# Turning the expert rows on VectorE in 32x32 squares instead of on TensorE

## The chip, the cores and the metric

The kernel runs on one core of a Trainium2 chip. The metric is device time in microseconds (us) of one execution; the kernel before takes 2286.07 us, the median of three runs (2285.0 to 2286.5). Lower is better. All data are float32 in HBM; the products on TensorE (PE) are split products, in which each operand is written as a high part (rounded to the type fp32r) and a low part (what the rounding left), and three of the four partial products are summed.

## The reference

The first half is an attention without a softmax over 8 batches of 2496 tokens, the second a mixture of 8 experts over all 19968 tokens, each sent to one expert:

```python
# attention: u, v (8, 2496, 256), z (8, 2496, 64)
scores = scale * np.matmul(z, z.transpose(0, 2, 1))     # scale = 1 / 2496
x = u * np.matmul(np.maximum(scores, 0.0) ** 2, v)       # then (19968, 256)
# mixture of experts: w_gate (256, 8), w1 (8, 256, 1024), w2 (8, 1024, 256)
logits = x @ w_gate + modality_bias[modality_id]
e_idx = np.argmax(logits, axis=1)
probs = np.exp(logits - logits.max(-1, keepdims=True)); probs /= probs.sum(-1, keepdims=True) + 1e-09
gate_w = probs[np.arange(N), e_idx]
for e in range(8):
    mask = e_idx == e
    out[mask] = gate_w[mask, None] * (np.maximum(x[mask] @ w1[e], 0.0) @ w2[e])
```

## The kernel before

**Phase 1** (from the start to about 1357 us) does the attention in 400 steps: 8 batches, 5 chunks of up to 512 query tokens in each, 10 steps of 256 key tokens in each chunk. A step's scores go through PE (`s`, L265), ScalarE (ACT) twice (`r`, L267 and L273), are split into `ah` (L280, on ACT or on VectorE (DVE), as a planner chooses) and `al` (L289, DVE), and are multiplied by `v` on PE (`acc`, L305). A finished chunk leaves its PSUM banks (L347, L351), is turned and multiplied by `u`, and stands in a buffer `x` of 512 rows of 258 numbers (256 values, the gate, the token number). DVE then makes the chunk's 32 dot products with `w_gate` (`logits`, L403: 128x256 each, two to a piece, 16 pieces). After a batch's last logits its routing follows, and each 128 rows of `x` are scattered by an indirect DMA from GpSimd (POOL) to their expert's rows in the HBM buffer `xs` (L516).

The order of DVE and ACT in phase 1 is made in Python, before the run, by a planner: `queue(first step, due step, pieces)` hands it pieces with the engine and an assumed cost, and in each step it places what is due and, where its clock for the engine has room, what is not yet due. The pieces that are due decide at which step the logits stand before or behind the next `al`.

**Phase 2** runs 39 full tiles of 512 tokens of one expert, numbered -4 to 34, then a quarter tile of 128 tokens and a short end that is left by branches. SyncE (SP) fetches a tile's rows from `xs` into `xg` by one DMA (L757: 128 partitions of four rows of 258 numbers, 4128 B each), and an expert's weights by two more (L775, L779), which ACT and DVE split (L795, L799). The expert products need the rows with their 256 values on the partitions: `turn` (L819) turns them on PE by eight products with the identity into two PSUM banks (`pt`), and `part_rows` makes `xh` (ACT, L827) and `xl` (DVE, L828) from these. In tile t this is done for tile t+1, behind step f = 1 (f = 5 in the tiles before 0).

A tile has eight steps f. `up(t, f)` is six products (L984) into a bank `ph`; ACT makes `hh` from it (L988), DVE `hl` (L989). Two steps later `down(t, f)` multiplies these by the second weights into four banks `po` (L997 with `hh`, L998 with `hl`, once for each 128 tokens). So step f puts on PE `up(f)` and four pairs of `down(f-2)`; behind step 7 come `down(6)` and `down(7)` for each bank, and `finish` scales the banks by the gate (ACT L1012, DVE L1014) and scatters them to the output (POOL L1016). In phase 2 the order on each engine is the order in which the code issues.

The seam between the phases: tile -4 starts as soon as its rows and weights are split, while the last chunk of batch 7 is still being evacuated, turned, multiplied (L351, L372), given its logits, routed and scattered between the steps of tiles -4 to -1. The tiles from 0 on may be fetched only after the last of these scatters.

## Time and profile before

| | |
|---|---|
| median of three runs | 2286.07 us |
| profiled execution, own time | 2288.12 us |
| its span, first to last instruction | 2286.2 us |
| PE busy | 2263.1 us, 99% |
| DVE busy | 1756.6 us, 77% |
| ACT busy | 1584.1 us, 69% |
| POOL busy | 364.6 us, 16% |
| 16 DMA engines, mean of the HBM traffic | 101 GB/s |
| mean granted TensorE clock | 0.997 of full |

Busy time is the time in which an engine executes; times are of the one profiled execution. The granted clock in a row of windows is a share of the full 2.4 GHz. In a list of waits "a <- b" means that the work named a could not start before b had ended. A number in brackets at the end of a timeline row is the time that the engine stood idle before it and what it waited for; a row without one followed the row before it on its engine at once. Matmuls of one bank overlap in a timeline: from one start to the next is what one costs.

### The profile page before, as it was taken

Reading aid. Unit: us, or ns where it says so; the run is one execution under the profiler, and the core shown is the slowest. Engines: PE = TensorE matmul, PEld = TensorE weight load, DVE = VectorE, ACT = ScalarE, POOL = GpSimd, SP = SyncE. Lnnn points to the kernel's source line nnn. Section 1 sums busy time; section 2 is a strip of 40 time slices with the busy share of each in tenths; the row PEclk is TensorE's granted clock in tenths of the full one; section 3 lists DMA queues with packets and bytes.
Section 4 is the critical chain, followed back from the end, with each engine's and each line's share of the span. In section 5 each row is a group of like instructions: output and inputs, shape, how many; then the busy total and the mean of one; then the engine's idle time right before and its main releaser. Section 6 shows DMA issues by size and latency. Waiting matters only on the chain.

```text
span 2286.2 us, 44695 instructions
## 1 busy us (share of the span) xinstructions
PE 2263.1 (99%) x17194; PEld 1945.6 (85%) x17194; DVE 1756.6 (77%) x4544; ACT 1584.1 (69%) x1957; POOL 364.6 (16%) x349
## 2 busy tenths in 40 slices
PE   9999999999999999999999999999999999999996
PEld 7789889889899899889888888888888888888885
DVE  6889989989989889889889997555555565656563
ACT  7888888888888888888888863545444544545452
POOL 0000210210220210210210413212121212121111
PEclk9999999999999999999999999999999999999998
DMA  9612112112112112112111122434343444434340
GB/s 303 226 33 66 47 47 78 38 53 71 41 52 70 41 60 62 52 50 64 49 43 33 58 93 91 169 118 148 129 145 133 136 141 131 146 124 154 116 155 22
DMA packets 101743, 216.62 MB, mean 95 GB/s; under 512 B 15472, under 2 KB 63216, under 8 KB 96656
## 3 DMA queue, kind: packets, MB, share of 16 engines
q1 hardware_dynamic: 86432, 172.48, 23.1%
q0 software_dynamic: 15088, 41.21, 4.9%
q8 instruction: 136, 2.23, 0.4%
q14 instruction: 87, 0.71, 0.1%
HBM read 168.23 MB, written 62.19 MB: 101 GB/s over the span
## 4 chain that ended last, share of the span: by engine, by line
PE 85%; DVE 10%; issue 3%; ACT 1%; DMA 0%; POOL 0%; DVEq 0%; POOLq 0%; ACTq 0%
PE acc L305 36%; PE ph L984 18%; PE po L997 12%; PE s L265 10%; PE po L998 6%; DVE spare L403 4%; DVE al L289 3%; PE pt L819 1%; DVE vl L240 1%; DVE ah L280 1%; PE po L381 1%; DVE x L351 1%; ACT r L267 1%; ACT r L273 0%; DVE x L391 0%
## 5 line engine op out<-in xcount | busy, mean ns | idle before, releaser
L267 ACT ACTIVATE r<-s 128x1024 f32<-128x1024 f32 (+1 forms) x400 | 403.8, 1010 | 199.5 <-PE s L265 194.8
L289 DVE TENSOR_TENSOR al<-r,ah 128x1024 fp32r<-128x1024 f32 (+1 forms) x360 | 431.3, 1198 | 102.0 <-ACT ah L280 86.7
L403 DVE SCALAR_TENSOR_TENSOR spare<-x,wgb 128x256 f32<-128x256 f32 x1280 | 462.8, 423 | 1.0
L305 PE MATMUL acc<-ah,vh 64*128 64x512 f32 (+1 forms) x3120 | 454.4, 384 | 0.9 <-DVE ah L280 0.9
L997 PE MATMUL po<-w,hh 128*128 128x512 f32 x1256 | 450.1, 393 | 0.0
L988 ACT ACTIVATE hh<-ph 128x512 fp32r<-128x512 f32 x312 | 186.8, 599 | 378.3 <-PE ph L984 374.0
L305 PE MATMUL acc<-ah,vl 64*128 64x512 f32 (+1 forms) x3120 | 445.6, 383 | 0.0
L305 PE MATMUL acc<-al,vh 64*128 64x512 f32 (+1 forms) x3120 | 444.5, 382 | 0.0
L984 PE MATMUL ph<-xh,w 128*128 128x512 f32 x1248 | 439.8, 398 | 0.5 <-DVE hl L989 0.3
L273 ACT ACTIVATE r<-r 128x1024 f32<-128x1024 f32 (+1 forms) x400 | 416.8, 1042 | 3.3
L989 DVE SCALAR_TENSOR_TENSOR hl<-ph,hh 128x512 fp32r<-128x512 f32 x312 | 215.6, 691 | 248.4 <-ACT hh L988 246.9
L516 POOL DMA_INDIRECT xs<-x,sloti x160 | 204.4, 1278 | 1028.1 <-DVE x L514 946.2
L305 PEld LDWEIGHTS acc<-ah,vh 64*128 64x128 f32 x3120 | 324.0, 184 | 48.3 <-ACT x L347 2.9
L305 PEld LDWEIGHTS acc<-al,vh 64*128 64x128 f32 x3120 | 324.7, 184 | 41.8
L305 PEld LDWEIGHTS acc<-ah,vl 64*128 64x128 f32 x3120 | 319.7, 185 | 45.1
L265 PE MATMUL s<-zm 64*128 64x512 f32 (+1 forms) x2400 | 352.6, 387 | 2.3 <-ACT r L267 2.3
L998 PE MATMUL po<-w,hl 128*128 128x256 f32 x1256 | 350.7, 279 | 0.0
L280 ACT CAST ah<-r 128x1024 fp32r<-128x1024 f32 (+1 forms) x289 | 294.8, 1020 | 0.0
L997 PEld LDWEIGHTS po<-w,hh 128*128 128x128 f32 x1256 | 235.4, 187 | 56.1
L984 PEld LDWEIGHTS ph<-xh,w 128*128 128x128 f32 x1248 | 234.0, 188 | 56.9 <-DVE hl L989 2.3
L265 PEld LDWEIGHTS s<-zm 64*128 64x128 f32 x2400 | 241.7, 185 | 32.9 <-ACT r L267 4.3
L1016 POOL DMA_INDIRECT out_dram<-y,ids x157 | 153.2, 976 | 720.5 <-DVE y L1014 694.8
(152 smaller groups left out, 1975.2 us busy)
## 6 DMA issues: line engine op xcount, KB each, us to landing
...
```

Source lines behind the costliest of these rows:

```text
L265: nc.tensor.matmul(out=s[:, t, :w], lhsT=lhs, rhs=mv[halves[t], ql, :w], start=n == 0, stop=n == 2)
L267: nc.scalar.activation(out=r[:, :, :w], in_=s[:, :, :w], func=AF.Relu, scale=INV)
L273: nc.scalar.square(out=a[:, :, :w], in_=a[:, :, :w])
L280: copy(out=ah[:, :, :w], in_=st_a[g][:, :, :w])
L289: nc.vector.tensor_tensor(out=al[:, :, :w], in0=a[:, :, :w], in1=ah[:, :, :w].bitcast(F32), op=ALU.subtract)
L305: nc.tensor.matmul(out=acc[b, c][r][dh][:, :w], lhsT=V[b, k // J][y][halves[r], k % J, dh * P:(dh + 1) * P], rhs=x[halves[r], k % 2, :w], ...
L403: nc.vector.scalar_tensor_tensor(out=spare[:, k % 2, :], in0=x[:, j, 0:D], scalar=1.0, in1=wgb[:, e, :], op0=ALU.mult, op1=ALU.mult, accum ...
L516: nc.gpsimd.indirect_dma_start(out=xs, out_offset=bass.IndirectOffsetOnAxis(ap=RT[b]["sloti"][:n, k:k + 1], axis=0), in_=x[:n, j, :], in_o ...
L984: nc.tensor.matmul(out=ph, lhsT=lhs, rhs=rhs[:, k, :], start=n == 0, stop=n == 3 * KD - 1)
L989: nc.vector.scalar_tensor_tensor(out=hl, in0=ph, scalar=0.0, in1=hh.bitcast(F32), op0=ALU.max, op1=ALU.subtract)
L997: nc.tensor.matmul(out=po[j], lhsT=hh[:, s], rhs=both, start=f == 0, stop=False, skip_group_check=True)
L998: nc.tensor.matmul(out=po[j][:, 0:D], lhsT=hl[:, s], rhs=w[:, 0, :], start=False, stop=f == KF - 1, skip_group_check=True)
```

## The change

The eight products with the identity, their two PSUM banks and the split from PSUM go. A tile's rows are now fetched by four DMAs, each of 32 partitions by 16 by 64 numbers (2048 pieces of 256 B in all), so that the 32x32 squares of the row matrix lie where one transposition of 128x1024 numbers by DVE, which turns each square in itself, brings the values onto the partitions (`turn_blocks`); a fifth DMA brings the gates and token numbers (512 pieces of 8 B). ACT makes the high part (`part_high`, 128x1024), DVE the low part (`part_low`, 128x1024). The values then stand on the partitions in another order, and the first weights are laid into HBM in that order, by two DMAs for an expert instead of one. The tile t+1 is turned behind step 6 of tile t and split behind step 7 (4 and 5 in tile -3). There are two buffers of `xg` instead of three, four of gates, seven of `x` instead of six, two of logits instead of one; the four PSUM banks that `ph` and `pt` shared two and two all belong to `ph`. In phase 1 the logits of a chunk are due by half a step each from step 8 of the next chunk on (before: step 6, and for a batch's last chunk a third of a step each from step 5; that stays for batch 6's last chunk and batch 7's second). The small tile `tt` is filled at the start. The diff, cut:

```diff
-            nc.sync.dma_start(out=w1s[e], in_=w1[e].rearrange("(k p) f -> p k f", p=P))
+            for k in range(KD):
+                nc.sync.dma_start(
+                    out=w1s[e, :, k, :].rearrange("(b q) f -> b q f", q=BLK),
+                    in_=w1[e].rearrange("(b k q) f -> k b q f", k=KD, q=BLK)[k],
+                )
...
-            x = rows.tile([P, J, XW], F32, tag="x", bufs=NCH + 1, name="x")
+            x = rows.tile([P, J, XW], F32, tag="x", bufs=NCH + 2, name="x")
...
-            LG[b] = rows.tile([P, NCOL, E], F32, tag="lg", bufs=1, name="lg")
+            LG[b] = rows.tile([P, NCOL, E], F32, tag="lg", bufs=2, name="lg")
...
-                    last = c == NCH - 1 or b == B - 1 and c == 1
-                    queue(g + NI + 2, g + NI + (5 + n // 3 if last else 6 + n // 2), dve(0.35 * LG_STEP, logits, b, c, n))
+                    hurry = b == B - 2 and c == NCH - 1 or b == B - 1 and c == 1
+                    queue(g + NI + 2, g + NI + (5 + n // 3 if hurry else 8 + n // 2), dve(0.35 * LG_STEP, logits, b, c, n))
...
-        k = fetched["n"] % 3
+        k = fetched["n"] % 2
-        xg = head[k // 2].tile([P, J, XW], F32R, tag=f"xg{k}", name="xg")[:, 0:nj, :].bitcast(F32)
+        xg = head[k].tile([P, T // BLK, KD * BLK], F32, tag=f"xg{k}", name="xg")[:, 0:nt // BLK, :]
+        side = small.tile([P, J, 2], F32, tag="gate", bufs=4, name="gate")[:, 0:nj, :]
-        i = ins_of(nc.sync.dma_start(out=xg, in_=src.rearrange("(p j) c -> p j c", j=nj)))
+        for b in range(P // BLK):
+            cols = slice(b * KD * BLK, (b + 1) * KD * BLK)
+            rows_of = src[:, cols].rearrange("(t i) c -> i t c", i=BLK)
+            dmas.append(nc.sync.dma_start(out=xg[b * BLK:(b + 1) * BLK], in_=rows_of))
+        dmas.append(nc.sync.dma_start(out=side, in_=src[:, D:XW].rearrange("(j p) c -> p j c", p=P)))
...
-    def turn_rows(t, dh):
-        pt = bank_tile([P, T], "pt")[:, 0:nj * P]
-        for j in range(nj):
-            nc.tensor.transpose(
...
-    def part_rows(x, dh, pt):
-        nc.scalar.copy(out=x[0][:, dh, :], in_=pt)
-        nc.vector.tensor_tensor(out=x[1][:, dh, :], in0=pt, in1=x[0][:, dh, :].bitcast(F32), op=ALU.subtract)
...
+    def turn_blocks(t):
+        side, xg = TL[t]
+        nt = xg.shape[1] * BLK
+        xt = turned.tile([P, KD, T], F32, tag="zm", bufs=NCH + 1, name="xt")[:, :, 0:nt]
+        TL[t] = (side, xt)
+        nc.vector.transpose(
+            out=xt.rearrange("p k (t i) -> p k t i", i=BLK), in_=xg.rearrange("p t (k c) -> p k t c", k=KD)
+        )
+    def part_high(t):
...
+        nc.scalar.copy(out=xh, in_=xt)
+    def part_low(t):
...
+        nc.vector.tensor_tensor(out=xl, in0=xt, in1=xh.bitcast(F32), op=ALU.subtract)
...
-    at(G - 5, turn_early, -EARLY)
-    queue(G - 4, G - 4, none(part_early, -EARLY))
+    queue(G - 6, G - 4, dve(1.2, turn_blocks, -EARLY), act(1.05, part_high, -EARLY), dve(1.25, part_low, -EARLY))
...
-    ps_h = ph2.enter_context(tc.tile_pool(name="ps_h", bufs=2, space=PSUM, reuse_waits="tile"))
-    bank.update(pool=ph2.enter_context(tc.tile_pool(name="ps_m", bufs=2, space=PSUM, reuse_waits="tile")), tag="m")
+    ps_h = ph2.enter_context(tc.tile_pool(name="ps_h", bufs=4, space=PSUM, reuse_waits="tile"))
+    bank.update(pool=ps_h, tag="h")
...
-            if f == (1 if t >= 0 else 5) and ahead and t + 1 in TL:
-                turn(t + 1)
+            if ahead and t + 1 in TL:
+                if f == turn_at(t):
+                    turn_blocks(t + 1)
+                if f == turn_at(t) + 1:
+                    part_high(t + 1)
+                    part_low(t + 1)
...
     for n in range(LGN):
-        between[0][2 + n * (KF - 2) // LGN].append(lambda n=n: logits(B - 1, NCH - 1, n))
+        put(2 + n // 2, lambda n=n: logits(B - 1, NCH - 1, n))
+    for slot, pieces in ((10, (route_logits, route_exp)), (11, (route_places,)), (13, (route_count,)), (14, (route_slots, route_gates))):
+        put(slot, *(lambda p=p: p(B - 1, LATE) for p in pieces))
+    for k in range(LATE.start, NCOL):
+        put(14 + k - LATE.start, lambda k=k: scatter(B - 1, k))
...
+    put(20, lambda: fetch_weights(0))
+    put(26, lambda: prefetch(-1), lambda: fetch_weights(1))
```

What moves on DVE shows best in three places. The first is a full tile of the steady part of phase 2. Before, from the end of one tile into the next (`y` is the last of `finish`, `hl` a step's low part, `xl` the next tile's rows, `w` a quarter of the next weights):

```order
L1014 SCALAR_TENSOR_TENSOR y<-po,xg,part_20535 128x256
L989 SCALAR_TENSOR_TENSOR hl<-ph,hh 128x512 x2
L828 TENSOR_TENSOR xl<-pt,xh 128x512 x2
L989 SCALAR_TENSOR_TENSOR hl<-ph,hh 128x512
L799 TENSOR_TENSOR w_0_18680<-w_0_18680 128x1024
L989 SCALAR_TENSOR_TENSOR hl<-ph,hh 128x512
```

Now, from the last quarter of the weights in step 5 to the end of the tile:

```order
L988 SCALAR_TENSOR_TENSOR hl<-ph,hh 128x512
L813 TENSOR_TENSOR w_2_19208<-w_2_19208 128x4x256
L988 SCALAR_TENSOR_TENSOR hl<-ph,hh 128x512
L831 STREAM_TRANSPOSE xt<-xg 128x1024
L988 SCALAR_TENSOR_TENSOR hl<-ph,hh 128x512
L843 TENSOR_TENSOR xl<-xt,xh 128x1024
L1006 CAST ids<-gate 128x4
```

The two `xl` behind `hl(1)` are gone; the transposition stands between `hl(6)` and `hl(7)`, and one `xl` of twice the size behind `hl(7)`.

The second place is the seam between the phases, on DVE: the end of the last `al` of phase 1 up to the first `hl` of tile -4 (`spare,lg` is a pair of logits for each two counted, `x<-acc` the evacuation of the last chunk). Before:

```order
L828 TENSOR_TENSOR xl<-pt,xh 128x512 x2
L291 TENSOR_TENSOR al<-r,ah 128x448
L292 TENSOR_TENSOR al<-r,ah 64x448
L403 SCALAR_TENSOR_TENSOR spare,lg<-x,wgb 128x256 x6
L799 TENSOR_TENSOR w_0_18680<-w_0_18680 128x1024 x2
L403 SCALAR_TENSOR_TENSOR spare,lg<-x,wgb 128x256 x2
L514 COPY x<-side 128x2
L799 TENSOR_TENSOR w_0_18681<-w_0_18681 128x4x256 x2
L351 TENSOR_TENSOR x<-acc,x 128x448 x2
L514 COPY x<-side 128x2
L403 SCALAR_TENSOR_TENSOR spare,lg<-x,wgb 128x256 x2
L989 SCALAR_TENSOR_TENSOR hl<-ph,hh 128x512 x3
```

Now (the transposition of tile -4 stands six rows earlier, in front of the last `al` but one):

```order
L288 CAST ah<-r 128x2x448
L299 TENSOR_TENSOR al<-r,ah 128x448
L300 TENSOR_TENSOR al<-r,ah 64x448
L411 SCALAR_TENSOR_TENSOR spare,lg<-x,wgb 128x256 x2
L813 TENSOR_TENSOR w_0_18690<-w_0_18690 128x1024
L843 TENSOR_TENSOR xl<-xt,xh 128x1024
L813 TENSOR_TENSOR w_0_18690<-w_0_18690 128x1024
L522 COPY x<-side 128x2
L813 TENSOR_TENSOR w_0_18691<-w_0_18691 128x4x256 x2
L359 TENSOR_TENSOR x<-acc,x 128x448 x2
L411 SCALAR_TENSOR_TENSOR spare,lg<-x,wgb 128x256 x10
L988 SCALAR_TENSOR_TENSOR hl<-ph,hh 128x512 x3
```

Ten logits instead of two stand between the evacuation and the first `hl`, and one `ah` has come to DVE.

The third place is the seam between two batches in phase 1, on DVE. Before, from the last logits of the batch to its routing (`bias` to `sh`):

```order
L403 SCALAR_TENSOR_TENSOR spare,lg<-x,wgb 128x256 x6
L289 TENSOR_TENSOR al<-r,ah 128x1024
L351 TENSOR_TENSOR x<-acc,x 128x512 x2
L403 SCALAR_TENSOR_TENSOR spare,lg<-x,wgb 128x256 x2
L280 CAST ah<-r 128x1024
L289 TENSOR_TENSOR al<-r,ah 128x1024
L426 TENSOR_TENSOR bias<-brow,mod_121 128x160
```

Now:

```order
L359 TENSOR_TENSOR x<-acc,x 128x512 x2
L297 TENSOR_TENSOR al<-r,ah 128x1024
L411 SCALAR_TENSOR_TENSOR spare,lg<-x,wgb 128x256 x8
L297 TENSOR_TENSOR al<-r,ah 128x1024
L399 TENSOR_TENSOR x<-po,ut 128x4x2x64 x2
L411 SCALAR_TENSOR_TENSOR spare,lg<-x,wgb 128x256 x2
L297 TENSOR_TENSOR al<-r,ah 128x1024
L411 SCALAR_TENSOR_TENSOR spare,lg<-x,wgb 128x256 x6
L434 TENSOR_TENSOR bias<-brow,mod_122 128x160
```

The last logits and the routing behind them have moved two steps back, and runs of up to eight logits now stand in front of an `al`.

## Rows read from the trace of the kernel before

**Rows 1.** Windows: length; PE, PEld, DVE, ACT, POOL busy us (instructions); clock; DMA share; GB/s.
```profile
350.00:700.00 350.00, 349.85 (x3243) 313.03 (x3241) 314.71 (x947) 299.64 (x331) 52.36 (x44) 1.00 0.18 58
...
1340.00:1370.00 30.00, 29.64 (x231) 25.35 (x228) 28.15 (x100) 16.34 (x22) 7.13 (x8) 1.00 0.13 46
...
1500.00:2240.00 740.00, 740.00 (x3847) 622.96 (x3847) 437.02 (x609) 366.19 (x578) 125.86 (x130) 1.00 0.40 137
```

**Rows 2.** Waits of PE, whole run, first and last of five: total us, times, longest.
```profile
PE s L265 <- ACT r L267: 2.3, 4, 1.1
...
PE po L381 <- DVE x L351: 0.3, 1, 0.3
```

**Rows 3.** Tile pt: instructions, ns min/median/max, first and last start.
```profile
L819 PE MATMUL pt<-ident,xg x314: 221/247/282, 1347.4 to 2240.8; 128*128 128x128 f32 x157
```

**Rows 4.** Timeline of PE in a tile: start us, duration, instruction.
```profile
1502.17 0.79 PE L819 MATMUL pt<-ident,xg 128*128 128x128 f32 x8
1502.80 0.47 PE L984 MATMUL ph<-xh,w 128*128 128x512 f32 x1
1503.11 0.39 PE L984 MATMUL ph<-xl,w 128*128 128x512 f32 x1
```

**Rows 5.** Chain of waits from 1500 us on: start us, us, what.
```profile
1522.61 2.80 PE ph L984 x12
...
1528.91 1.40 PE ph L984 x6
...
1545.69 2.79 PE ph L984 x12
...
2215.01 2.80 PE ph L984 x12
```

**Rows 6.** Costliest groups of the page: busy us, mean ns | idle before, releaser.
```profile
L289 DVE TENSOR_TENSOR al<-r,ah 128x1024 fp32r<-128x1024 f32 (+1 forms) x360 | 431.3, 1198 | 102.0 <-ACT ah L280 86.7
L403 DVE SCALAR_TENSOR_TENSOR spare<-x,wgb 128x256 f32<-128x256 f32 x1280 | 462.8, 423 | 1.0
L280 ACT CAST ah<-r 128x1024 fp32r<-128x1024 f32 (+1 forms) x289 | 294.8, 1020 | 0.0
```

**Rows 7.** Lines L280, L462 and L488: ns min/median/max, first and last start.
```profile
L280 DVE CAST ah<-r x111: 615/689/700, 9.8 to 1326.5; 128x1024 fp32r<-128x1024 f32 x95, 128x896 fp32r<-128x896 f32 x16
...
L462 DVE TENSOR_TENSOR_SCAN run<-reset,hot x9: 491/491/492, 228.9 to 1389.7; 128x160 f32<-128x160 f32 x9
...
L488 DVE TENSOR_TENSOR base<-pc,base x17: 154/166/167, 238.4 to 1392.0; 128x8 f32<-128x8 f32 x17
```

**Rows 8.** Timeline of PE, ACT and DVE behind up(7) of tile 34.
```profile
2256.39 0.39 PE L997 MATMUL po<-w,hh 128*128 128x512 f32 x1
2256.59 0.60 ACT L988 ACTIVATE hh<-ph 128x512 fp32r<-128x512 f32 x1 [2.20 <-PE ph L984]
...
2257.22 0.69 DVE L989 SCALAR_TENSOR_TENSOR hl<-ph,hh 128x512 fp32r<-128x512 f32 x1 [2.11 <-ACT hh L988]
...
2258.37 0.28 PE L998 MATMUL po<-w,hl 128*128 128x256 f32 x1
```

**Rows 9.** DMA queues of the page: packets, MB, share of 16 engines' span.
```profile
q1 hardware_dynamic: 86432, 172.48, 23.1%
```

**Rows 10.** Windows, a stretch of small packets; columns as in rows 1.
```profile
15.00:18.50 3.50, 3.50 (x34) 3.02 (x32) 2.13 (x3) 2.20 (x3) 0.00 (x0) 1.00 0.65 53
```

**Rows 11.** Timeline of SP, the DMAs of that stretch.
```profile
13.99 2.86 SPq L187 DMA_DIRECT2D mi<-in_moe_modality_id_dram  x4
```

**Rows 12.** Timeline of DVE and PE at the seam of the phases.
```profile
1361.27 1.28 DVE L989 SCALAR_TENSOR_TENSOR hl<-ph,hh 128x512 fp32r<-128x512 f32 x2
1362.00 0.50 PE L984 MATMUL ph<-xh,w 128*128 128x512 f32 x1 [0.33 <-DVE hl L989]
```

**Rows 13.** Timeline of DVE and PE at a seam of batches: `al`, its first use.
```profile
547.97 1.22 DVE L289 TENSOR_TENSOR al<-r,ah 128x1024 fp32r<-128x1024 f32 x1
...
554.50 0.81 PE L305 MATMUL acc<-al,vh 64*128 64x512 f32 x4
```

More of the change, by code (lines that the diff above doesn't have):

```diff
@@ L52, in tile_attention_moe @@
     XW = D + 2
+    BLK = 32
     CAP = N
@@ L97, in tile_attention_moe, with iota_f32 @@
     late = []
-    def iota_f32(shape, pattern, base, mult, name):
+    def iota_f32(shape, pattern, base, mult, name, pool=small):
         n = math.prod(shape[1:])
         i = raw.tile([P, n], I32, tag=name + "_i", name=name + "_i")
-        f = small.tile(shape, F32, name=name)
+        f = pool.tile(shape, F32, name=name)
         nc.gpsimd.iota(i, pattern=pattern, base=base, channel_multiplier=mult)
@@ L105, in iota_f32 @@
         return f
[L107 removed]
+    col = iota_f32([P, P], [[1, P]], 0, 0, "col", raw)
     part = iota_f32([P, 1], [[1, 1]], 0, 1, "part")
@@ L113, in tile_attention_moe @@
     base0 = small.tile([P, E], F32, name="base0")
+    tt = small.tile([1, MAXT, 1], F32, name="tt")
     reset = small.tile([P, E, NCOL], F32, name="reset")
@@ L131, in prep_constants @@
         nc.vector.tensor_copy(out=base0, in_=base)
+        nc.vector.tensor_copy(out=tt[:, :, 0], in_=col[0:1, 0:MAXT])
     blank = []
@@ L616, in over @@
             return x.rearrange("p (o e) -> p o e", o=1).broadcast_to(shape)
-        tt = small.tile([1, MAXT, 1], F32, name="tt")
-        nc.vector.tensor_copy(out=tt[:, :, 0], in_=col[one, 0:MAXT])
         ge = t3("p_ge")
@@ L740, in tile_attention_moe, with wait_rows @@
     data = mybir.DependencyInfo(mybir.DependencyClass.Sync, mybir.DependencyReason.DATA)
-    def wait_rows(i):
+    def wait_rows(dmas):
         for s in scatters[ready["n"]:]:
-            tc.add_manual_dep(i, s.name, data, reason="rows of tokens")
+            for i in dmas:
+                tc.add_manual_dep(i, s.name, data, reason="rows of tokens")
         ready["n"] = len(scatters)
@@ L809, in begin @@
         fetch_weights(-1)
[L810 to L848 removed]
+    def turn_blocks(t):
[7 more added lines that the diff above has]
+    def part_high(t):
+        side, xt = TL[t]
+        xh, xl = (turned.tile([P, KD, T], F32R, tag="zm", bufs=NCH + 1, name=n)[:, :, 0:xt.shape[2]] for n in ("xh", "xl"))
+        nc.scalar.copy(out=xh, in_=xt)
+        TL[t] = (side, xh, xl, xt)
+    def part_low(t):
+        side, xh, xl, xt = TL[t]
+        nc.vector.tensor_tensor(out=xl, in0=xt, in1=xh.bitcast(F32), op=ALU.subtract)
+        TL[t] = (side, xh, xl)
+    def turn(t):
+        for f in (turn_blocks, part_high, part_low):
+            f(t)
     at(EG + 2, begin)
@@ L1064, in run_quarter, with turn_at @@
         finish(t, po, f"out{t}{part}")
+    def turn_at(t):
+        return 4 if t == 1 - EARLY else KF - 2
     def run_tile(t, ahead, extra={}, part=""):
-        if not isinstance(TL[t], tuple):
+        if len(TL[t]) < 3:
             turn(t)
@@ L1093, in tile_attention_moe, with put @@
     between[0][2] += [lambda: take_last_rows(B - 1, NCH - 1)]
+    slots = [(n, f) for n in range(EARLY) for f in range(KF)]
+    def put(slot, *pieces):
+        n, f = slots[slot]
+        between[n][f] += pieces
     for n in range(LGN):
-        between[0][2 + n * (KF - 2) // LGN].append(lambda n=n: logits(B - 1, NCH - 1, n))
-    planning = plan()
-    slots = [(n, f) for n in range(EARLY) for f in range(KF)][KF:]
-    for k, pieces in ((0, (route_logits, route_exp)), (1, (route_places,)), (3, (route_count, route_slots, route_gates))):
-        n, f = slots[k]
-        between[n][f] += [lambda p=p: p(B - 1, LATE) for p in pieces]
-    for k, (n, f) in zip(range(LATE.start, NCOL), slots[4:]):
-        between[n][f].append(lambda k=k: scatter(B - 1, k))
-    for n, f in slots[5:13]:
-        between[n][f].append(lambda: next(planning, None))
-    n, f = slots[13]
-    between[n][f] += [lambda: fetch_weights(0)]
-    between[3][0] += [lambda: fetch_weights(1)]
+        put(2 + n // 2, lambda n=n: logits(B - 1, NCH - 1, n))
[3 more added lines that the diff above has]
+        put(14 + k - LATE.start, lambda k=k: scatter(B - 1, k))
+    planning = plan()
+    for slot in (15, 16, 17, 18, 18, 19, 19, 20):
+        put(slot, lambda: next(planning, None))
+    put(20, lambda: fetch_weights(0))
+    put(26, lambda: prefetch(-1), lambda: fetch_weights(1))
     ph2.enter_context(tc.manual_schedule(engines={ET.PE, ET.Activation, ET.DVE, ET.Pool, ET.SP}))
     for t in range(-EARLY, UNC):
-        if t > -EARLY:
-            prefetch(t)
+        prefetch(t)
         if t == 0:
```

38 lines of the change are left out of this document (8 added, 30 removed).

## The prediction

> **What bounds the kernel now.** I read the windows first, then what PE waits for, then the chain of waits, and last the timelines around the places that the change touches. In both phases PE is busy to the last tenth of a microsecond: 349.85 of 350 us in a stretch of the attention, 740.00 of 740 in the expert tiles, at a granted clock of 1.00 (its level of 2.4 GHz) in both, while in the tiles DVE is busy for 59%, ACT for 49%, and the DMA engines for 0.40 [rows 1]. The list of PE's waits on other engines has five entries, the largest 2.3 us in all, the smallest 0.3 [rows 2]. So PE's own instructions set the end: taking work from PE shortens the run by what that work takes in PE's row, as long as nothing becomes late; work added to DVE, ACT or the queues costs nothing while they keep ahead.
>
> **What is removed.** PE loses 314 products with the identity, eight in each of 39 tiles and two in the quarter tile [rows 3]. Their price is not the duration of one (247 ns), since they overlap, but what they shift: eight start at 1502.17 us and the next product at 1502.80, so 0.63; that product takes 0.31 to the next start [rows 4] instead of 1.40 / 6 = 0.23 [rows 5], so 0.7 in all. The chain says the same another way: a tile's period is 1545.69 - 1522.61 = 23.08 us, and from step 3 to the end of the tile there are six steps of (1545.69 - 1528.91) / 6 = 2.797; eight of them are 22.38, which leaves 0.70 for the turn. The period holds to the last tile: (2215.01 - 1522.61) / 30 = 23.08 [rows 5]. Two of the 39 turns belong to the seam of the phases and are counted there; the other 37 give 25.9 us, the two small ones in the quarter tile some 0.3 (a quarter of eight at 0.70, rounded up for the bubble that a short group leaves).
>
> The Trainium skill ("TensorE: Matmul & The Clock Gate", Part 4: PE-mode transpose) gives about 275 ns for one transposition of 128x128 in a kernel. By it eight would cost 2.2 us and 39 tiles 86 us, three times my sum. The trace disagrees: the durations are near that figure (247 ns), but PE starts one every 0.08 us, so only the row's 0.70 can come back.
>
> **What is added in a tile.** No transposition by DVE stands in the trace of before. By the nearest rows it lies between 0.69 us (a cast of 128x1024 on DVE, the fastest row of that size) and 2.3 us (the dearest operation for each number is the scan: (491 - 166) ns / 152 numbers = 2.1 ns, for 1024 numbers 2.2 us, with its fixed part 2.3) [rows 7]. I take 1.2, the row of `al`, a subtraction of that size (1.198) [rows 6]: it too streams 1024 float32 in each partition. The low part becomes one subtraction of 1.2 instead of two of half the size; ACT's high part 1.02 [rows 6] instead of two halves. DVE thus gets about 1 us more a tile, 64% instead of 59% of the period: cover enough on average.
>
> It must also fit where it stands. It is issued between `hl(6)` and `hl(7)`, so `hl(7)` and PE's `down(7)` queue behind it. In tile 34 up(7) ends at 2256.39; `hh(7)` is ready 0.80 later, `hl(7)` starts at 2257.22, 0.83 behind up(7), and DVE has stood idle 2.11 before it; `hl(7)` ends at 2257.91 and PE needs it at 2258.37, 1.98 behind up(7) [rows 8]. So the transposition may take 2.11 + 0.46 = 2.57 us before PE waits. At 1.2 it costs nothing, even at 2.3. The low part follows at 0.83 + 0.69 = 1.5 us or, if ACT's cast of 1.02 behind `hh(7)` ends later, at 1.8, and ends at 3.1 behind up(7); the next tile's up(0) comes 4.2 behind it (twelve pairs of down at 0.35) and wants `xl` one product later. More than 1 us is left.
>
> **The transfers.** A fetch becomes 2048 pieces of 256 B and 512 of 8 B, instead of 128 of 4128 B. The mean packet of SP's queue now takes 23.1% x 16 x 2286.2 us / 86432 = 97.8 ns for 2.0 KB [rows 9]. The other end is a stretch in which four DMAs of 32 KB in 32-byte pieces ran [rows 11]: 0.65 x 16 x 3.5 us [rows 10] / 4096 = 8.9 ns or less for one, if all of them fell into it. On a line between the two a piece of 256 B takes 19 ns, and a fetch 2048 x 19 / 16 + 512 x 8.9 / 16 = 2.7 us of all 16 engines, where now it takes some 1.6 (516 KB at the mean rate). The bounds are 1.4 (all at 8.9) and 15.6 us (all at 97.8). With 0.40 x 23.08 = 9.2 us of DMA in a tile now, the tile has 10.3 of 22.38, at the upper bound 23.2, and only there would DMA be the limit. I take 10.3. The fetch is issued at the start of the tile before the one in which the rows are turned, so it has more than a period to land. SP issues five DMAs for one, and nothing in a steady tile waits for SP.
>
> **The seam of the phases.** DVE is busy for 28.15 of 30 us around the seam [rows 1]; tile -4's `hl(0)` follows the row before it at once, at 1361.27, and up(2) of tile -4 waits for it: it starts at 1362.00, after 0.33 of waiting [rows 12]. Four banks in `ph`'s pool instead of two do not help there, since two of them are just being used for the last chunk's rows. In the order of after DVE has as many logits as before, 20, between the third `al` from the end and `hl(0)`; but now the transposition stands there too (+1.2) and one cast `ah` (+0.7) [rows 7], and one `xl` of twice the size costs some 0.2 less than two (1.2 against 2 x 0.69, the price of `hl`, which has that size) [rows 8]. That is +1.7, so up(2) comes 1.7 us later. Of the two turns in front of tile -3, the one in phase 1 gives nothing back, since DVE sets the end there; the other gives 0.7. So tile -3 starts 1.0 later. In tile -4 four logits (1.4 us) stand beside the transposition between `hl(6)` and `hl(7)`, 2.6 us in a room of 2.57 (no wait worth counting), and four more before `xl`, which ends at about 4.7 behind up(7), where PE wants it at 4.4: one more wait, 0.3.
>
> **Phase 1.** PE's work is the same there. DVE's pieces stand in another order: at a seam of batches up to eight logits (2.9 us) and a cast now precede an `al`. In the steady part an `al` is ready long before its use: 547.97 + 1.22 = 549.19 against 554.50, 5.3 us [rows 13], and before an `al` DVE waits 86.7 us in all for ACT's `ah` [rows 6], so it is mostly ahead. The work that comes in front of one `al` over a seam adds up to 4.8 us at most by my count of the order, less than 5.3. I cost it at nothing; if the cover is gone, each seam would cost a microsecond or so. The laying of the first weights in two DMAs and the extra buffers cost no engine time.
>
> **Sum.** -25.9 - 0.3 + 1.0 + 0.3 = -24.9 us. The profiled execution took 2288.12 us, 1.9 over its span, and would take 2263.2; it stands 2.05 above the median of the runs, which becomes 2286.07 - 24.9 = 2261.2, so 2261.
>
> **The rivals.**
> (B) The transposition overruns its room. Over 2.57 us, each microsecond more delays `down(7)` in 38 tiles. For it speaks that nothing in the trace prices moving numbers between partitions; against it that even the scan's price fits. It turns slower than before from 2.57 + 25 / 38 = 3.2 us on; at 4.6 us (twice the bound) it is 38 x 2.0 = +77, 2338 us.
> (C) The small pieces make DMA the limit. At the upper bound of 97.8 ns the tile has 23.2 us of DMA, about the period of now: no gain, 2286 to 2290. At 120 ns it would be 26.8 us and some 2400. For it: SP's mean packet does take 97.8 ns; against: that packet is eight times longer, and the 32-byte pieces went through in 8.9. The Trainium skill ("DMA: Bandwidth & Descriptors", Specifications) wants transfers of 512 B or more for the full rate, and says that below this a read-modify-write takes place; by that rule the 2048 pieces of 256 B and the 512 of 8 B are the weak point. No run here shows it yet.
> (D) The new order of phase 1 makes `al` or an evacuation late at the seams: seven seams at 0.5 to 1.5 us, 2264 to 2272. For it: the runs of eight logits; against: the 5.3 us.
> (E) The gain comes, but the first fetches of tiles 0 and 1, which stand behind the last scatters on POOL's queue and now come later, hold PE once for 5 to 20 us: 2266 to 2281.
>
> **How the numbers follow.** My forecast: 0.72, own range 2257 to 2266 (the seam's 1.7 could be 0 or 4, the start could give back some waits). B 0.06, C 0.06, D 0.10, E 0.06. About 0.2%, 4.6 us, is what a measurement of this kernel can tell from no change. Faster by more: the forecast, D, most of E (0.04) and of C a third (0.02), 0.88; within: the rest of E and C's bound, 0.05; slower: B and the far part of C, 0.07. The range, 2257 to 2270, holds the forecast and most of D, 0.8; B and C are outside.
>
> **What would show it.** Right: no row of `pt`; in the chain, periods of 22.38 us; a transposition of about 1.2 us, and no PE wait on `hl` in the tiles; PE still busy for 349.8 of 350 us in phase 1; a wait of some 2 us before up(2) of tile -4; a DMA share of about 0.45 in the tiles. Wrong: PE waiting for `hl` once a tile (B), a DMA share near 1 and transpositions waiting for `xg` (C), entries of `acc` on `al` seven times (D), one long wait near 1445 us (E).

## The result, and the profile after

The changed kernel takes 2263.62 us (median of 4 runs, 2263.0 to 2264.21), the kernel before 2286.28 in the runs beside it: a ratio of 0.9902, 95% interval 0.9885 to 0.9919, 22.7 us faster. The forecast was 2261, range 2257 to 2270. The profiled execution took 2264.21 us, its span 2262.4.

The windows of the changed kernel, columns as in [rows 1], which they answer to:

```profile
350.00:700.00 350.00, 350.00 (x3250) 341.33 (x3248) 318.20 (x956) 297.92 (x329) 54.49 (x45) 1.00 0.23 74
...
1340.00:1370.00 30.00, 26.91 (x184) 23.18 (x182) 26.17 (x84) 11.29 (x15) 5.42 (x6) 0.94 0.26 55
...
1500.00:2210.00 710.00, 710.00 (x3530) 595.34 (x3529) 464.41 (x598) 357.32 (x534) 120.64 (x124) 1.00 0.48 139
```

PE is full in both phases as before, DVE has 65% in the tiles (59 before), DMA 0.48 (0.40). The seam of the phases has become worse: PE is idle for 3 us there and the granted clock is 0.94. The list of PE's waits says on what, and is otherwise that of [rows 2]:

```profile
PE ph L983 <- DVE hl L988: 3.1, 1, 3.1
PE s L273 <- ACT r L275: 2.3, 4, 1.1
```

The new tile's instructions (ns min/median/max, first and last start), and the timeline of DVE and ACT in tile 1, which answers to [rows 8]:

```profile
L831 DVE STREAM_TRANSPOSE xt<-xg x40: 434/1235/1245, 1340.2 to 2231.2; 128x1024 f32<-128x1024 f32 x39, 128x256 f32<-128x256 f32 x1
```

```profile
1487.34 1.23 DVE L831 STREAM_TRANSPOSE xt<-xg 128x1024 f32<-128x1024 f32 x1
...
1488.94 0.60 ACT L987 ACTIVATE hh<-ph 128x512 fp32r<-128x512 f32 x1 [2.24 <-PE ph L983]
...
1489.57 0.69 DVE L988 SCALAR_TENSOR_TENSOR hl<-ph,hh 128x512 fp32r<-128x512 f32 x1 [0.99 <-ACT hh L987]
```

A transposition takes 1.235 us, and DVE still waits 0.99 for ACT behind it: `hl(7)` is not late.

The chain of waits, which gave the periods before [rows 5], does not run through the tiles in this trace; the periods are read from ACT's first `hh` of each tile (of its timeline, tiles 2 to 5):

```profile
1494.58 0.60 ACT L987 ACTIVATE hh<-ph 128x512 fp32r<-128x512 f32 x1 [0.93 <-PE ph L983]
...
1517.02 0.60 ACT L987 ACTIVATE hh<-ph 128x512 fp32r<-128x512 f32 x1 [0.92 <-PE ph L983]
...
1539.59 0.60 ACT L987 ACTIVATE hh<-ph 128x512 fp32r<-128x512 f32 x1 [0.92 <-PE ph L983]
...
1562.20 0.60 ACT L987 ACTIVATE hh<-ph 128x512 fp32r<-128x512 f32 x1 [0.93 <-PE ph L983]
```

22.44, 22.57, 22.61, and so on in turn to the last tile: three values that follow the three buffers of weights, 22.54 on average, where eight plain steps of before are 22.38.

By the starts of these instructions (`r<-s` of a step in phase 1, the first `hh` of a tile) in both traces, the 23.8 us by which the span is shorter lie here:

| stretch | before | after | difference | forecast |
|---|---|---|---|---|
| start to step 10 | 41.12 | 39.15 | -1.97 | 0 |
| steps 10 to 399 | 1303.92 | 1301.27 | -2.65 | 0 |
| step 399 to tile -4 | 14.20 | 13.43 | -0.77 | } +1.0 |
| tile -4 | 24.83 | 28.25 | +3.42 | } |
| tiles -3 to -1 | 70.73 | 67.27 | -3.46 | -1.8 |
| tiles 0 to 33 | 784.72 | 766.42 | -18.30 | -23.8 |
| tile 34 to the end | 46.68 | 46.61 | -0.07 | -0.3 |

The sum agrees with the forecast to 1.1 us (-23.8 against -24.9), its parts do not. Some 2.0 us at the start are most likely chance (see "The start" below), and without them the stretches come to -21.8. Steps 10 to 399 gained 2.65 us that were not forecast, and tiles 0 to 33 gained 5.5 us less than forecast. The experiments were made for the parts.

### The profile page after: what moved, and what is told of

It reads as the page before. It is cut to its first block, busy times and chain, and to the rows that moved or that the text cites. A ratio compares the mean times of both kernels' runs of the same rounds, so it can differ in the third digit from the quotient of the medians.

```text
span 2262.4 us, 44477 instructions
## 1 busy us (share of the span) xinstructions
PE 2237.1 (99%) x16880; PEld 2025.0 (90%) x16880; DVE 1805.4 (80%) x4550; ACT 1573.2 (70%) x1911; POOL 368.7 (16%) x349
## 4 chain that ended last, share of the span: by engine, by line
PE 58%; issue 26%; DMA 9%; POOL 3%; DVE 2%; ACT 1%; POOLq 0%; SPq 0%; DVEq 0%; ACTq 0%
PE acc L313 42%; PE s L273 11%; DMA out_dram<-y,ids 9%; POOL out_dram L1015 3%; PE ph L983 1%; PE po L996 1%; PE po L389 1%; DVE spare L411 1%; PE po L997 1%; DVE al L297 0%; POOL xs L524 0%; ACT r L275 0%; DMA xs<-x,sloti 0%; DVE x L359 0%; PE warm L863 0%
## 5 line engine op out<-in xcount | busy, mean ns | idle before, releaser
L313 PE MATMUL acc<-ah,vh 64*128 64x512 f32 (+1 forms) x3120 | 498.0, 385 | 0.8 <-DVE ah L288 0.8
L313 PE MATMUL acc<-ah,vl 64*128 64x512 f32 (+1 forms) x3120 | 490.2, 383 | 0.0
L313 PE MATMUL acc<-al,vh 64*128 64x512 f32 (+1 forms) x3120 | 488.5, 383 | 0.1
L983 PE MATMUL ph<-xh,w 128*128 128x512 f32 x1248 | 431.2, 396 | 3.1 <-DVE hl L988 3.1
L313 PEld LDWEIGHTS acc<-ah,vh 64*128 64x128 f32 x3120 | 386.3, 185 | 19.2 <-ACT x L355 1.7
L313 PEld LDWEIGHTS acc<-al,vh 64*128 64x128 f32 x3120 | 383.5, 185 | 17.0 <-DVE al L297 0.5
L313 PEld LDWEIGHTS acc<-ah,vl 64*128 64x128 f32 x3120 | 382.4, 185 | 16.8
L273 PE MATMUL s<-zm 64*128 64x512 f32 (+1 forms) x2400 | 391.5, 387 | 2.3 <-ACT r L275 2.3
L273 PEld LDWEIGHTS s<-zm 64*128 64x128 f32 x2400 | 294.2, 185 | 16.1 <-ACT r L275 4.2
L288 ACT CAST ah<-r 128x1024 fp32r<-128x1024 f32 (+1 forms) x283 | 288.2, 1018 | 0.0
```

The lines of the kernel that those rows point to most:

```text
L273: nc.tensor.matmul(out=s[:, t, :w], lhsT=lhs, rhs=mv[halves[t], ql, :w], start=n == 0, stop=n == 2)
L288: copy(out=ah[:, :, :w], in_=st_a[g][:, :, :w])
L313: nc.tensor.matmul(out=acc[b, c][r][dh][:, :w], lhsT=V[b, k // J][y][halves[r], k % J, dh * P:(dh + 1) * P], rhs=x[halves[r], k % 2, :w], ...
L983: nc.tensor.matmul(out=ph, lhsT=lhs, rhs=rhs[:, k, :], start=n == 0, stop=n == 3 * KD - 1)
```

## The experiments

The medians of the kernel before in the runs beside them are 2286.6 to 2286.8. A time with a ratio behind it is the median of four executions (of ten in the last experiment); a time without one is a single execution.

**Phase 1: the due steps.** The changed kernel with the old due steps.

```diff
-                    hurry = b == B - 2 and c == NCH - 1 or b == B - 1 and c == 1
-                    queue(g + NI + 2, g + NI + (5 + n // 3 if hurry else 8 + n // 2), ...
+                    hurry = c == NCH - 1 or b == B - 1 and c == 1
+                    queue(g + NI + 2, g + NI + (5 + n // 3 if hurry else 6 + n // 2), ...
```

> The changed kernel with the due steps of the logits put back (a batch's last chunk from step 5 by a third of a step each, others from step 6). Theory: phase 1 gained 0.45 us at each of six seams of batches, because the evacuation of the last chunk no longer stands on DVE behind six hurried logits and an al, and PE's turn of that chunk no longer waits for it; put back, ACT's first r of step 65 of batches 1 to 6 comes 0.45 later against the steps before it, phase 1 is 2.7 us longer, the run 2265 to 2268. Rival: the gain comes from the further buffers of x and logits, or from the start of the run alone; then the seams keep their times to 0.1 us, and the run 2263 to 2264.

Measured: 2270.15, above the expected 2265 to 2268. From step 10 to step 399 it takes 0.6 us more than the kernel before, where the changed kernel takes 2.65 less: 3.3 us lost, and none of the six seams has its gain. (In the changed kernel it is 0.7 us at the first and 0.4 to 0.5 at each of the others, some 3.2 in all; about 0.5 is lost elsewhere in phase 1.) The timelines of PE at the seam behind batch 1, and DVE's evacuation of the chunk that ends there, the first of batch 2, show the wait. Before:

```profile
387.93 0.84 PE L305 MATMUL acc<-al,vh 64*128 64x512 f32 x4
388.84 0.71 PE L381 MATMUL po<-ident,x 64*128 64x64 f32 x16
...
387.49 1.29 DVE L351 TENSOR_TENSOR x<-acc,x 128x512 f32<-128x512 f32 x2
```

In the changed kernel:

```profile
385.23 0.83 PE L313 MATMUL acc<-al,vh 64*128 64x512 f32 x4
385.69 0.67 PE L389 MATMUL po<-ident,x 64*128 64x64 f32 x13
...
383.72 1.29 DVE L359 TENSOR_TENSOR x<-acc,x 128x512 f32<-128x512 f32 x2 [1.17 <-ACT x L355]
```

With the old due steps:

```profile
387.82 0.85 PE L313 MATMUL acc<-al,vh 64*128 64x512 f32 x4
388.75 0.71 PE L389 MATMUL po<-ident,x 64*128 64x64 f32 x16
```

The same four products are followed after 0.91, 0.46 and 0.93 us. Before, DVE's evacuation (two instructions, from 387.49 to 388.78) ends just before 388.84: PE's turn of the finished chunk waited for it, since six hurried logits and an `al` stood ahead of it on DVE. In the changed kernel DVE waits 1.17 us for ACT's part and evacuates at once. The theory holds in phase 1, and the further buffers of `x` and logits, which this run keeps, do not give the gain. The wait of 0.45 stands in no list of waits: the modelled end of the products (0.84 us for four that take 0.46) covers it. Of the 5.9 us by which the run lies over the changed kernel's profiled execution, 3.3 are in phase 1, 1.7 the start (below), and 0.9 lie behind phase 1 and outside the span.

**The tile: two PSUM banks for `ph`.**

```diff
-    ps_h = ph2.enter_context(tc.tile_pool(name="ps_h", bufs=4, space=PSUM, reuse_waits="tile"))
-    bank.update(pool=ps_h, tag="h")
+    ps_h = ph2.enter_context(tc.tile_pool(name="ps_h", bufs=2, space=PSUM, reuse_waits="tile"))
+    bank.update(pool=ph2.enter_context(tc.tile_pool(name="ps_m", bufs=2, space=PSUM, reuse_waits="tile")), tag="m")
```

> The changed kernel with two PSUM banks for ph instead of four (the other two serve only the last chunk of phase 1, as before). Theory: up(2) of a tile must wait until hl(0) has left its bank, some 0.3 us; before, the turn on PE stood just there and hid it, so with two banks the turn's removal would have given only 0.4 a tile. A tile's period goes from 22.54 to 22.84 us on average, with an entry of some 0.3 us before up(2), and the run to 2273 to 2275. Rival: PE has no such wait (the list of its waits before names none in the tiles), period 22.54, run 2263 to 2265.

Measured: 2272.58, periods of 22.58 to 22.89 us, 22.78 on average, some 0.25 more (expected: 22.84). PE's timeline at the start of a tile:

```profile
1540.80 0.63 PE L983 MATMUL ph<-xh,w 128*128 128x512 f32 x2
1541.27 0.39 PE L983 MATMUL ph<-xl,w 128*128 128x512 f32 x1
1541.50 0.91 PE L983 MATMUL ph<-xh,w 128*128 128x512 f32 x2
1542.25 0.39 PE L983 MATMUL ph<-xl,w 128*128 128x512 f32 x1
```

Two products take 0.47 to the next start in the first row and 0.75 in the third, whose second product is the first of up(2): 0.28 of waiting for the bank of up(0), again not listed (an entry had been expected). The kernel before has the same wait in tile -2, where the turn stands at another step and does not cover it:

```profile
1409.02 0.91 PE L984 MATMUL ph<-xh,w 128*128 128x512 f32 x2
1409.77 0.40 PE L984 MATMUL ph<-xl,w 128*128 128x512 f32 x1
```

Again 0.75. So the turn of before stood on a wait: without the two further banks its removal would have given an estimated 0.70 - 0.28 = 0.42 a tile. In tiles -3 to -1 of before both were paid, which is why these three gave 1.15 us each.

**The seam: the logits in front of `hl(0)`.** The ten logits that the planner still holds at the end of phase 1 are taken out and put into later steps of the tiles.

```diff
+        held = [q[2][0] for q in waiting if q[2][0][2] is logits]
+        waiting = [q for q in waiting if q[2][0][2] is not logits]
         while waiting:
...
+    for slot, (_, _, f, args) in zip((3, 4, 5, 8, 9), held):
+        put(slot, lambda f=f, args=args: f(*args))
```

> The changed kernel with the ten logits that stand between the evacuation of the last chunk and hl(0) of tile -4 put behind it, a pair each in steps 3, 4, 5 of tile -4 and 0, 1 of tile -3. Theory: hl(0) of tile -4 comes 3.45 us earlier, up(2) no longer waits (3.09 us in the changed kernel), and TensorE's clock, which falls to 0.50 of full for 3.2 us just behind that wait, stays at 1.00 (1.6 us more): the run is 4 to 5 us shorter, 2259. Rival: DVE's work is only moved, and the same wait comes two or three steps later, at hl(3) to hl(5): gain below 1 us, 2263.

Measured: 2260.43 (ratio 0.9884, 0.9868 to 0.9901), 3.2 us less, between the two. The wait of 3.1 is gone from PE's list and tile -4 takes 23.4 us instead of 28.3; but tile -3, whose first steps got six logits each, takes 23.5 instead of 22.7. The wait cost more than its 3.1 us: in the changed kernel's profile the clock, which is 1.00 up to it, falls behind it. Windows of the changed kernel:

```profile
1360.00:1361.00 1.00, 1.00 (x5) 0.78 (x4) 0.00 (x0) 0.00 (x0) 0.00 (x0) 0.84 0.74 157
1361.00:1362.00 1.00, 1.00 (x4) 0.81 (x4) 0.35 (x1) 0.60 (x1) 0.00 (x0) 0.50 1.07 207
...
1364.00:1365.00 1.00, 1.00 (x5) 0.81 (x5) 0.91 (x6) 0.00 (x0) 0.00 (x0) 0.95 1.19 224
```

0.50 is 1.2 GHz instead of 2.4. Tile -4 is 4.85 us longer than the 23.4 that it takes without the wait, 3.1 of them the wait itself and 1.7 this stretch, some 3.4 us at half the clock. With the late logits, without the wait, the clock does not fall:

```profile
1360.00:1365.00 5.00, 5.00 (x27) 4.27 (x26) 5.00 (x24) 1.20 (x2) 0.00 (x0) 1.00 0.64 116
```

But the wait does not always bring the fall. Eight of the traces have it. In six the clock falls behind it, in the run with three transpositions (below), where a wait of 1.5 us stands ahead of it, already during it. In the run with two banks for `ph` PE waits just as long, the clock stays at 1.00, and tile -4 takes 26.80 us instead of 28.25:

```profile
1359.56 0.50 PE L983 MATMUL ph<-xh,w 128*128 128x512 f32 x1 [3.10 <-DVE hl L988]
...
1360.00:1365.00 5.00, 5.00 (x27) 4.18 (x26) 3.20 (x11) 1.20 (x2) 0.00 (x0) 1.00 0.88 157
```

What decides it stays open; that part of the loss is in one execution and not in another.

**The tile: 32 bytes.** The remaining 0.16 us a tile went by the buffer of the weights. The buffers of the second phase that lie behind those of the first had moved by 4384 bytes (one more `x`, 4128, one more buffer of logits, 640, and four of gates, 128, less 512 for `col`, which now lies elsewhere), which is not a multiple of 64: `hh` and `hl`, at a multiple of 64 bytes in a partition before, lay 32 off, and the weights of tiles 0, 1, 3, 4, ..., 32 off before, lay at a multiple. (These places are worked out from the sizes of the buffers in the code; no trace shows an address.) A pad of 32 bytes puts all of these back; it moves some smaller buffers of the phase as well.

```diff
     mp = ph2.enter_context(tc.tile_pool(name="mp", bufs=2, reuse_waits="tile"))
+    pad = mp.tile([P, 8], F32, tag="pad", bufs=1, name="pad")
+    nc.vector.memset(pad, 0.0)
```

> The changed kernel with 32 bytes of padding in front of the second phase's buffers: hh, hl and the weights of two of three tiles lie 32 bytes further, at the same place within 64 bytes as in the kernel before. Theory: the 0.16 us by which a tile's period (22.57, 22.60, 22.45 in turn) exceeds eight plain steps of before (22.38) comes from where these buffers lie, since it sits in the products with hh and hl and goes by the weights' three buffers: periods go to 22.38 or below, the run to 2257 to 2259. Rival: place has nothing to do with it (DVE's transposition, the small transfers or TensorE itself), periods stay at 22.54 on average, run 2263 to 2264.

Measured: 2260.37 (0.9885, 0.9869 to 0.9902). ACT's first `hh` of tiles 2 to 4:

```profile
1494.40 0.60 ACT L989 ACTIVATE hh<-ph 128x512 fp32r<-128x512 f32 x1 [0.92 <-PE ph L985]
...
1516.80 0.60 ACT L989 ACTIVATE hh<-ph 128x512 fp32r<-128x512 f32 x1 [0.92 <-PE ph L985]
...
1539.20 0.60 ACT L989 ACTIVATE hh<-ph 128x512 fp32r<-128x512 f32 x1 [0.92 <-PE ph L985]
```

22.40 in every tile, where the forecast had 22.38; the run lies 1.4 us above the expected 2257 to 2259. The theory holds for the tiles: the missing 0.14 to 0.16 comes from where the buffers lie. Two more runs took the shifts apart: a pad in front of the weights alone (`wp`), and both pads.

```diff
     wp = ph2.enter_context(tc.tile_pool(name="wp", bufs=1, reuse_waits="tile"))
+    pad2 = wp.tile([P, 8], F32, name="pad2")
+    nc.vector.memset(pad2, 0.0)
```

> The changed kernel with 32 bytes of padding in front of the weights of tiles 0, 1, 3, 4, ... alone: these come to the place within 64 bytes that they had before, hh and hl stay 32 bytes off. Theory W (the place of the weights decides): all periods like those of the third weights' buffer, which lies so already, 22.45, run about 2260. Theory H (the place of hh and hl decides): periods stay 22.57, 22.60, 22.45, run 2263 to 2264. If both count, all periods are 22.45 and only both shifts give 22.40.

> The changed kernel with hh and hl shifted by 32 bytes, the weights of two tiles of three by 64: hh and hl at the place within 64 bytes of before, these weights at that of the changed kernel. Theory H: all periods 22.40, run 2260. Theory W: two of three periods 22.54 to 22.60, the third 22.40, run 2263.

Measured: 2258.42 and 2258.08, both below what either theory had. With the pad in front of the weights alone:

```profile
1496.07 0.60 ACT L989 ACTIVATE hh<-ph 128x512 fp32r<-128x512 f32 x1 [0.93 <-PE ph L985]
...
1518.39 0.60 ACT L989 ACTIVATE hh<-ph 128x512 fp32r<-128x512 f32 x1 [0.93 <-PE ph L985]
```

22.32 in all tiles. With both pads (tiles 1 to 4):

```profile
1473.69 0.60 ACT L991 ACTIVATE hh<-ph 128x512 fp32r<-128x512 f32 x1 [0.92 <-PE ph L987]
...
1495.94 0.60 ACT L991 ACTIVATE hh<-ph 128x512 fp32r<-128x512 f32 x1 [0.93 <-PE ph L987]
...
1518.36 0.60 ACT L991 ACTIVATE hh<-ph 128x512 fp32r<-128x512 f32 x1 [0.93 <-PE ph L987]
...
1540.60 0.60 ACT L991 ACTIVATE hh<-ph 128x512 fp32r<-128x512 f32 x1 [0.92 <-PE ph L987]
```

22.25, 22.42, 22.24. Neither theory W nor H. By the places worked out above, with `hh` and `hl` at 0 within 64 bytes a tile took 22.24 with its weights at 0 and 22.40 with them at 32; with `hh` and `hl` at 32 it took 22.59 with its weights at 0, and 22.32 or 22.44 with them at 32, according to where the other weights lay. That led to a third theory, that alike is best, tried below.

**The room for the transposition.** The padded kernel with the transposition done three times.

```diff
-        nc.vector.transpose(
-            out=xt.rearrange("p k (t i) -> p k t i", i=BLK), in_=xg.rearrange("p t (k c) -> p k t c", k=KD)
-        )
+        for _ in range(3):
+            nc.vector.transpose(
+                out=xt.rearrange("p k (t i) -> p k t i", i=BLK), in_=xg.rearrange("p t (k c) -> p k t c", k=KD)
+            )
```

> The padded kernel with the transposition done three times in a row, 3 x 1.23 = 3.7 us between hl(6) and hl(7). Theory of the prediction: the room is 2.57 us, so PE waits 1.1 us for hl(7) in each of the tiles; a period of 23.5 instead of 22.40, the run some 40 us longer, 2300. Rival: PE has more room than the rows of before showed (under 0.3 us a tile, run below 2272), or the clock falls behind each wait and the tile takes 24 us or more (run above 2320).

Measured: 2311.43, where 2300 was expected. From PE's list of waits, and from DVE's and PE's timeline in a tile:

```profile
PE po L1000 <- DVE hl L991: 37.0, 38, 2.3
```

```profile
1547.19 3.80 DVE L832 STREAM_TRANSPOSE xt<-xg 128x1024 f32<-128x1024 f32 x3
...
1551.62 0.39 PE L1000 MATMUL po<-w,hl 128*128 128x256 f32 x1 [0.92 <-DVE hl L991]
```

The periods are 23.60 instead of 22.40: +1.20 for 3.80 us of transposition, so the room is 3.80 - 1.20 = 2.6, where the prediction had 2.57. The run is some 11 us longer than expected: 8.6 of them are in tiles -4 and -3, where DVE has logits beside the transposition and which take 35.0 and 24.7 us instead of 28.3 and 22.7, and most of the rest is 1.20 a tile instead of 1.1. From 1500 us on the clock is 1.00 in spite of 1.2 us lost to waiting in each tile.

**The transfers.** The padded kernel with one DMA for a tile's rows.

```diff
-        for b in range(P // BLK):
-            cols = slice(b * KD * BLK, (b + 1) * KD * BLK)
-            rows_of = src[:, cols].rearrange("(t i) c -> i t c", i=BLK)
-            dmas.append(nc.sync.dma_start(out=xg[b * BLK:(b + 1) * BLK], in_=rows_of))
+        whole = src.rearrange("(p j) c -> p (j c)", j=nj)[:, 0:2 * nt]
+        dmas.append(nc.sync.dma_start(out=xg.rearrange("p t c -> p (t c)"), in_=whole))
```

> The padded kernel (e8) with a tile's rows fetched by one DMA of 128 pieces of 4096 B, the gates as in the changed kernel; the rows then lie wrongly and the expert products work on other numbers, at the same size. Theory of the prediction: the 2048 pieces of 256 B are hidden; periods stay 22.40, the run within 1 us of the padded kernel but for the start, 2258 to 2261, while the DMA share in the tiles falls by about 0.05 (1.1 us of 22.4). Rival: the small pieces slow the transfers of weights or the writes of the output enough to be felt: periods below 22.40 or a run of 2256 and less.

Measured: 2261.62, periods of 22.40. The window of the tiles, with one DMA:

```profile
1500.00:2210.00 710.00, 710.00 (x3553) 596.11 (x3552) 467.97 (x601) 360.33 (x538) 120.94 (x124) 1.00 0.42 138
```

and in the padded kernel with its small pieces:

```profile
1500.00:2210.00 710.00, 710.00 (x3554) 596.04 (x3553) 467.51 (x603) 360.58 (x540) 121.48 (x125) 1.00 0.48 138
```

The pieces of 256 B cost 0.06 x 22.4 = 1.3 us of the 16 engines in a tile more than the large ones (the prediction: 2.7 - 1.6 = 1.1, with the 512 pieces of 8 B, which both kernels have) and no time of PE. The run is 2.15 us over the padded kernel's profiled execution (2259.47), 2.0 of them at the start.

**The start.** In the windows of the traces the clock from 10 to 14 us is 1.00 in six of the thirteen kernels and 0.57 to 0.60 in the other seven, with no pattern in the edits: kernels whose first steps are the same fall on both sides. Before:

```profile
10.00:12.00 2.00, 1.47 (x8) 1.19 (x10) 1.70 (x2) 1.97 (x3) 0.00 (x0) 0.65 1.04 426
12.00:14.00 2.00, 2.00 (x12) 1.60 (x10) 1.59 (x3) 1.81 (x3) 0.00 (x0) 0.50 0.96 395
```

In the changed kernel:

```profile
10.00:12.00 2.00, 1.93 (x16) 1.28 (x16) 1.35 (x2) 1.97 (x4) 0.00 (x0) 1.00 1.05 421
12.00:14.00 2.00, 2.00 (x22) 1.59 (x20) 1.97 (x3) 1.17 (x3) 0.00 (x0) 1.00 0.99 408
```

Step 10 comes at 38.9 to 39.5 us where it is 1.00 and at 40.9 to 41.2 where it is not. So it most likely belongs to the execution and not to the kernel, and blurs comparisons of single runs by some 2 us. No kernel has two traces to show it; but 13 executions of the kernel before in one batch lie at 2285.8 to 2286.7 or at 2287.8 to 2289.0, with none between.

**A faster version.** The pad of the first kind, and the held logits at steps 0, 1, 3, 4, 5 of tile -4.

```diff
-    for slot, (_, _, f, args) in zip((3, 4, 5, 8, 9), held):
+    for slot, (_, _, f, args) in zip((0, 1, 3, 4, 5), held):
```

> The changed kernel with the 32 bytes of padding and with the ten logits in front of hl(0) of tile -4 moved behind hl(0), hl(1) and into steps 3, 4 and 5 of tile -4, a pair each, none into tile -3. Theory: in the first try the six logits a step in tile -3 made its hl late and took back 1.9 of the 5 us won in tile -4; DVE has idle time between hl(0) and hl(2) of tile -4 for four of them. Tile -4 takes 23.2 us (28.3 with the logits in front), tile -3 22.4 to 22.8, the full tiles from 0 on 22.40: the run 2255 to 2256.5. Rival: DVE is full from hl(0) to the routing whatever the order, and the wait returns as late hl in tile -4 or -3: 2257 to 2259.

Measured: 2255.67 (0.9862, 0.9845 to 0.9878). Tile -4 23.40 (expected: 23.2), tile -3 22.72, those from -1 on 22.40, and no entry of `hl` in PE's list.

The same with both pads and one more behind the third weights' buffer, which lies at the right end of the memory and so moves down by 32 bytes:

```diff
         weight_tiles(pool, 0)
+        pad0 = pool.tile([P, 8], F32, name="pad0")
+        nc.vector.memset(pad0, 0.0)
```

> The version with the late logits (e9) and all of hh, hl and the three weights' buffers at multiples of 64 bytes. Theory: a period depends on whether hh, hl and the weights lie alike within 64 bytes: both at 0 gave 22.24 (two tiles of three in e11), both at 32 gave 22.32, hh and hl at 0 with the weights at 32 gave 22.40, the reverse 22.59. With all at 0 every tile from 0 on takes 22.24 us, 0.16 less than in e9, 5.8 us over 36 tiles: the run about 2250. Rival: the 22.24 came from the change between unlike buffers from tile to tile; then 22.3 to 22.4, the run 2253 to 2256.

Measured: 2251.57 (0.9841, 0.9825 to 0.9857), the fastest of all, 12 us below the changed kernel. Tiles 1 to 4:

```profile
1469.06 0.60 ACT L995 ACTIVATE hh<-ph 128x512 fp32r<-128x512 f32 x1 [0.92 <-PE ph L991]
...
1491.29 0.60 ACT L995 ACTIVATE hh<-ph 128x512 fp32r<-128x512 f32 x1 [0.91 <-PE ph L991]
...
1513.75 0.60 ACT L995 ACTIVATE hh<-ph 128x512 fp32r<-128x512 f32 x1 [0.93 <-PE ph L991]
...
1535.98 0.60 ACT L995 ACTIVATE hh<-ph 128x512 fp32r<-128x512 f32 x1 [0.92 <-issue]
```

22.23, 22.46, 22.23: the third buffer's tiles did not come down with the others, though by the sizes in the code it lies at a multiple of 64 now. So "alike is best" holds for two buffers and fails for the third. The kernel before with the same two pads for the weights:

> The kernel before with two paddings of 32 bytes, which bring the three weights' buffers to multiples of 64 bytes, where hh and hl lie already. Theory: the same 0.16 us a tile as in e11, periods 22.92 instead of 23.08, the run some 6 us shorter, 2280 to 2281. Rival: the place matters only where TensorE runs without the turn's gap and with four banks; then 23.08 and 2286.

Measured: 2285.46 (0.9993, 0.9983 to 1.0002, ten runs), no difference; periods of 22.99, 23.03 and 23.11 in turn, 23.04 on average against 23.08. The theory (22.92) fails; the place acts there too, but by 0.04, not 0.16. What rule it follows stays open: shown is that shifts of 32 and 64 bytes move a tile by up to 0.35 us (22.24 to 22.59), not which accesses meet.

## Why the prediction was right, and where its steps were not

- **PE sets the end** in the tiles and in phase 1: right. PE is busy for 710.00 of 710 us, and what was taken from it came back, but for what the next points say.
- **0.70 a tile for the turn**: right as the price of the eight products, mis-sized as the gain. Measured 0.54 in tiles 0 to 33. The step "the other 37 give 25.9" did not have two things. The buffers' place takes 0.14 to 0.16 back (22.40 with the pad), which is the whole shortfall. And under the turn stood a wait of 0.28 for the bank of up(0), which would have made the shortfall an estimated 0.44 a tile; the two further banks bought it off, of which the prediction said only that they do not help at the seam.
- **Tiles -3 to -1**: mis-sized the other way, 1.15 each instead of 0.6 to 0.7, since the turn and the wait for the bank were both paid there.
- **The transposition, 1.2 us in a room of 2.57**: right, 1.235 and, by the kernel with three, 2.6. Rival B's price a microsecond was right too (1.20 a tile for 1.23 over the room); its place was not reached.
- **The transfers, 2.7 us a fetch and hidden**: right that they are hidden, and somewhat small in size. The DMA share of 0.48 is 10.8 us a tile (forecast 10.3), and with one DMA the period is the same, so rival C fell. The Trainium skill ("DMA: Bandwidth & Descriptors", Specifications) wants 512 B for the full rate. The trace agrees in that 2048 pieces of 256 B took 1.3 us of DMA time a tile more than 128 pieces of 4096 B; it did not bear on the end.
- **The seam: up(2) 1.7 us later against phase 1**: right as far as it went. `hl(0)` starts at 1358.50 instead of 1361.27, 2.8 earlier where step 399 is 4.6 earlier: 1.85 later against it.

```profile
1358.50 1.28 DVE L988 SCALAR_TENSOR_TENSOR hl<-ph,hh 128x512 fp32r<-128x512 f32 x2
1359.23 0.51 PE L983 MATMUL ph<-xh,w 128*128 128x512 f32 x1 [3.09 <-DVE hl L988]
```

  These answer to [rows 12]. The wait grew from 0.33 to 3.09, where some 2 us were forecast, since PE came to it earlier by more than DVE did. What was missed is that the clock can fall behind such a wait, another 1.7 us in this execution. So tile -3 came 2.65 later against phase 1, not 1.0; in the run with two banks, where the clock did not fall, it came 1.2 later.
- **Phase 1 at nothing**: wrong, and it is what made the sum come out. The prediction asked only whether an `al` would be late in the new order. What gained was the evacuation, which PE's next turn waits for: some 0.5 us at each of six seams. The list of PE's waits held a sign of it: its last entry, 0.3 us once [rows 2], is this wait at the first of the six seams.

```profile
220.80 0.71 PE L381 MATMUL po<-ident,x 64*128 64x64 f32 x16 [0.30 <-DVE x L351]
```

  At the other five it has no entry, so that the list shows 0.3 of some 3 us that came back there. Rival D, the loss there, did not come, nor did rival E: PE's list has no long wait near 1445 us.
- **The start**, -2.0 in the two profiles, goes with the clock there and, as far as the traces tell, not with the change. The profiled executions differ by 23.9, the medians by 22.7.

So the total came near because errors offset each other, which is luck. The 2.65 us of unforecast gain in phase 1 stand against 5.5 missing in tiles 0 to 33, and 1.65 more won in tiles -3 to -1 against 1.65 lost at the seam. Without the start the stretches come to -21.8, 3.1 short of the forecast; by the medians it is 2.2 short.
